# A gated feed-forward block on one core: the down projection from seven block products

## The chip, the cores and the metric

The kernel runs on one core of a Trainium2 chip. The metric is the device time of one execution in microseconds, as the median of several runs. The engines are TensorE (PE, with its weight loads, PEld), VectorE (DVE), ScalarE (ACT), GpSimd (POOL) and SyncE (SP), which here only issues DMAs.

## The reference

A transformer block with 2048 tokens, model width 576 and feed-forward width 4608, all in 32-bit floating point:

```
h = layernorm(x) * (1 + ca) + sa
x = x + ga * attention(h)            # 32 heads of 18, four segments of 512 tokens, with a memory
h = layernorm(x) * (1 + cb) + sb
x = x + gb * ((silu(h @ w_gate) * (h @ w_up)) @ w_down)
```

`sa, ca, ga, sb, cb, gb` are rows of width 576 from `silu(c) @ w_mod`. The change concerns the last line.

## The kernel before, in words

**Products.** Each factor of an accurate product is split in two: a high part (`wh`, `ah`, `dh`, type fp32r) and the remainder (`wl`, `al`, `dl`). A product is then three matmuls: high x high, high x low, low x high. The high part is a cast on ACT, the remainder a subtraction on DVE.

**Stages.** First come layernorm, the projections and the memory. Then attention: 32 units of four heads (segment s, eighth q), as a software pipeline whose order is written out by hand. `PAT` holds four rows (even and odd units, q under 4 and from 4 on) of eleven slots; in each slot the next part of `p2_step` (scores, exponent on ACT, mask on POOL) and of `p1_seq` (row maxima of the unit after the next) is issued, and then the events that the slot names: `V` the product of probabilities and values (`av`), `m` and `n` the transposed maxima, their way through DRAM and `load_m`, `M` the output projection, and so on. `load_stack` on SP's queue brings queries and keys three units ahead.

**Feed-forward.** The 4608 columns are 18 pairs of two blocks of 128. The tokens are worked in two halves of 1024 (t = 0, 1), each as two blocks of 512. For each half and pair, gate (z = 0) and up (z = 1) are a 2x2 by 2x2 block product (two token blocks, two halves of the width 576, two column blocks) made from seven products instead of eight (Strassen and Winograd's form): `y` holds the seven sums of token blocks, `O` the four weight blocks and the three sums that POOL forms from them (`sum_o`), in each half anew. That is 14 steps k per pair. In a step, `prep_w` splits the weights of the step seven ahead, `prod` issues seven matmuls of 512 columns into a PSUM bank of its own (four banks in turn), and DVE adds the banks up (`T[0]`, `T[1]`) and finishes a result (`fin`): for gate ACT applies silu, for up DVE multiplies, and the product is split into `ah`, `al`.

**Down** is plain: `down(t, p, i)` takes token tile i of 128 (eight per half), issues 2 x 6 matmuls of 288 columns with the pair's down weights `dh`, `dl`, and DVE adds the bank to the accumulator `acc[i]`, which was loaded with the residual. Eight such steps for the pair before are issued after products 4 to 11. The down weights are loaded in each half, multiplied by the row gb (`gbB`) on POOL, and split.

**Beside it.** In the first half a second preparation (`prep2`, one yield in each of steps 4 to 13) computes the operands `y` of the second half and keeps them in DRAM (`yD`); at the change of half `load_y` brings each as soon as the last product with the old one has been issued. All DMAs here go through SP's queue, in program order; an engine, too, takes its instructions in program order.

## Time and profile before

| | |
|---|---|
| Time, median of 3 runs | 1944.75 us (1941.69 to 1944.93) |
| Profiled execution, span (the only time the profile has of it) | 1946.8 us |
| PE busy | 1901.2 us |
| PEld busy | 1593.1 us |
| DVE busy | 1533.1 us |
| ACT busy | 824.8 us |
| POOL busy | 1020.6 us |
| Mean granted TensorE clock | 0.993 |

Busy times are sums over stages that differ. A row of a group reads: line, engine, operation, output<-inputs, shapes, count | busy us, mean ns of one | idle time of the engine just before, and what ended it. A row of the timeline reads: start, length, engine, line, operation, count. A matmul's length includes its way through the pipeline, so that the pitch of matmuls is read from their starts.

### The profile page before, as it was taken

How to read it: one execution, taken by the hardware profiler on the slowest of the kernel's cores; microseconds unless marked ns; L12 is line 12 of the kernel's file. 1: busy time of each engine (PE TensorE's matmuls, PEld its weight loads, DVE VectorE, ACT ScalarE, POOL GpSimd, SP SyncE). 2: the span in 40 equal slices, each digit the busy share in tenths (PEclk: the TensorE clock that was granted, in tenths of full speed). 3: DMA queues.
4: the chain of work that ended last, by engine and by line, in shares of the span. 5: the costliest groups of instructions: out<-in, count | busy, mean ns of one | idle time of the engine just before them, and what ended most of it. 6: DMA issues, size and time to landing. Idle time of an engine off the chain costs nothing.

```text
span 1946.8 us, 31901 instructions
## 1 busy us (share of the span) xinstructions
PE 1901.2 (98%) x11119; PEld 1593.1 (82%) x11119; DVE 1533.1 (79%) x3218; ACT 824.8 (42%) x1652; POOL 1020.6 (52%) x1396
## 2 busy tenths in 40 slices
PE   7999999999999899999999999999999999999999
PEld 4887865676766678888888888888888888888888
DVE  6575257878786999898898988979888888878886
ACT  2222256767667434344344343433333333333332
POOL 5322235455544866556565565556565564655551
PEclk9999999999999899999999999999999999999999
DMA  7776564444443332232222222174211211112111
GB/s 207 244 227 233 203 204 140 131 139 150 136 128 125 92 135 101 89 106 80 80 106 83 82 84 78 60 264 146 74 62 45 74 62 59 60 62 74 62 57 50
DMA packets 114354, 223.59 MB, mean 115 GB/s; under 512 B 22992, under 2 KB 40784, under 8 KB 112720
## 3 DMA queue, kind: packets, MB, share of 16 engines
q1 hardware_dynamic: 111936, 215.61, 34.2%
q0 software_dynamic: 576, 5.11, 0.7%
q8 instruction: 88, 1.44, 0.3%
q10 hardware_dynamic: 1680, 0.82, 0.2%
q14 instruction: 74, 0.61, 0.1%
HBM read 161.11 MB, written 60.36 MB: 114 GB/s over the span
## 4 chain that ended last, share of the span: by engine, by line
PE 88%; DVE 4%; DMA 4%; ACT 1%; issue 1%; POOL 1%; SPq 1%; POOLq 0%; ACTq 0%; DVEq 0%
PE M L1090 39%; PE pd L1152 23%; PE pp L93 4%; PE s L576 4%; PE av L596 4%; PE s L174 4%; PE pv L93 3%; PE pw L694 2%; DMA O<-in_wgu_dram 1%; DMA mD<-mr 1%; PE pn L765 1%; PE pm L429 1%; PE px L617 1%; PE pr L346 1%; DVE y L923 1%
## 5 line engine op out<-in xcount | busy, mean ns | idle before, releaser
L1090 PE MATMUL M<-y,wh 128*128 128x512 f32 x2520 | 792.0, 393 | 5.0 <-DVE cu L1106 2.1
L1090 PEld LDWEIGHTS M<-y,wh 128*128 128x128 f32 x2520 | 473.7, 188 | 101.7 <-issue 3.9
L1067 POOL TENSOR_TENSOR wh<-O,wh 32x128 fp32r<-32x128 f32 x504 | 296.6, 593 | 423.0 <-ACT wh L1065 271.3
L1090 PE MATMUL M<-y,wl 128*128 128x512 f32 x1008 | 394.7, 392 | 0.0
L1059 POOL TENSOR_TENSOR O<-O 128x384 f32<-128x384 f32 x288 | 315.4, 1095 | 75.0 <-DMA O<-in_wgu_dram 42.9
L1152 PE MATMUL pd<-dh,ah 128*128 128x288 f32 x1152 | 340.3, 295 | 0.2 <-DVE acc L1155 0.2
L1152 PE MATMUL pd<-dl,ah 128*128 128x288 f32 x1152 | 340.3, 295 | 0.0
L1152 PE MATMUL pd<-dh,al 128*128 128x288 f32 x1152 | 340.1, 295 | 0.0
L1110 ACT CAST ah<-sg 128x512 fp32r<-128x512 f32 x144 | 89.5, 621 | 547.8 <-DVE sg L1107 422.0
L1155 DVE TENSOR_TENSOR acc<-acc,pd 128x576 f32<-128x576 f32 x288 | 216.5, 752 | 111.8 <-PE pd L1152 108.4
L1066 DVE TENSOR_TENSOR wl<-O,wh 128x256 fp32r<-128x256 f32 x504 | 286.2, 568 | 6.0 <-ACT wh L1065 5.2
L179 DVE CUSTOM_DVE_ANT_0 junk<-s,tri 128x256 bf16<-128x256 f32 (+3 forms) x512 | 228.7, 487 | 77.2 <-PE s L174 69.8
L1065 ACT CAST wh<-O 128x384 fp32r<-128x384 f32 x504 | 242.8, 507 | 0.0
L1152 PEld LDWEIGHTS pd<-dl,ah 128*128 128x128 f32 x1152 | 217.4, 189 | 11.8
L1152 PEld LDWEIGHTS pd<-dh,ah 128*128 128x128 f32 x1152 | 216.7, 188 | 11.6 <-DVE acc L1155 0.6
L579 ACT ACTIVATE Pt<-s 128x512 f32<-128x512 f32 (+1 forms) x352 | 186.5, 559 | 88.1 <-PE s L576 72.0
L1152 PEld LDWEIGHTS pd<-dh,al 128*128 128x128 f32 x1152 | 216.6, 188 | 0.0
L1090 PEld LDWEIGHTS M<-y,wl 128*128 128x128 f32 x1008 | 190.0, 188 | 29.6
L1102 ACT ACTIVATE sg<-sg 128x512 f32<-128x512 f32 x144 | 91.2, 633 | 222.7 <-DVE sg L1101 222.7
L576 PE MATMUL s<-qs,ks 110*128 110x512 f32 (+2 forms) x384 | 150.5, 409 | 5.7 <-DMA qs<-mD 4.4
L174 PE MATMUL s<-ks,qs 108*128 108x256 f32 (+3 forms) x512 | 141.2, 327 | 3.3 <-DMA ks<-kD 1.4
L583 POOL TENSOR_SCALAR_AFFINE_SELECT Pt<-Pt 128x512 f32<-128x512 f32 x128 | 81.6, 648 | 100.6 <-ACT Pt L579 100.2
(428 smaller groups left out, 2836.6 us busy)
## 6 DMA issues: line engine op xcount, KB each, us to landing
O<-in_wgu_dram SPq DMA_DIRECT2D x72, 768.0 KB
ks<-kD SPq DMA_DIRECT2D x68, 216.0 KB
qs<-qD SPq DMA_DIRECT2D x68, 216.0 KB
kD<-fh SPq DMA_DIRECT2D x16, 512.0 KB
qD<-fh SPq DMA_DIRECT2D x16, 512.0 KB
yD<-st SPq DMA_DIRECT2D x28, 256.0 KB
y<-yD SPq DMA_DIRECT2D x7, 1024.0 KB
wml<-in_w_mod_dram SPq DMA_DIRECT2D x24, 216.0 KB
```

The source lines that it names most:

```text
L93: nc.tensor.matmul(ps, lhsT=a, rhs=b, start=(k == 0), stop=(k == 13))
L174: nc.tensor.matmul(bank[:, n * (h - h0):n * (h - h0) + n], lhsT=qst[b][0:108, h, 128 * i:128 * i + 128], rhs=kst[b][0:108, h // 2, 0:n], s ...
L179: nc.vector.tensor_tensor_reduce(junk[:, :n], bank[:, n * (h - h0):n * (h - h0) + n], tri[:, L - n:], 1.0, -3e38, op0=ALU.add, op1=ALU.max ...
L576: nc.tensor.matmul(bank[:, n * (g - h):n * (g - h + w)].rearrange("p (a b) -> p a b", a=w), lhsT=kst[u % NB][0:110, g // 2, 128 * j:128 * ...
L579: nc.scalar.activation(pt[:, h:h + per, :n], bank[:, :n * per].rearrange("p (a b) -> p a b", a=per), AF.Exp, scale=SCALE)
L1059: nc.gpsimd.tensor_tensor(o[:, d], o[:, a], o[:, b], op=op)
L1065: nc.scalar.copy(wh, o)
L1066: later.append(lambda: nc.vector.tensor_tensor(wl, o[:, 0:2], f32(wh[:, 0:2]), op=ALU.subtract))
L1067: later.append(lambda: nc.gpsimd.tensor_tensor(wh[32:64, 2], o[32:64, 2], f32(wh[32:64, 2]), op=ALU.subtract))
L1090: nc.tensor.matmul(bank, lhsT=a, rhs=b, start=(n == 0), stop=(n == 6))
L1152: nc.tensor.matmul(pd[:, h, :288], lhsT=a[:, tk], rhs=w[:, f, sl], start=(k == 0), stop=(k == 5))
L1155: nc.vector.tensor_tensor(o, o, pd[:, :, :288], op=ALU.add)
```

## The change

**Down from seven products.** The four results of a pair (two token blocks, two column blocks) and the four 128x288 blocks of its down weights are combined like gate and up. `sum_a` forms four sums of the results on POOL; `prep_a` splits seven operands instead of four; `prep_d` splits seven weight blocks of 288 columns; `down(t, p, c)` issues 14 chunks of six matmuls of 288 columns, `CH` of them after each step, and each chunk is added by DVE to one of seven accumulators `acc[1..7]`. At the end of a half `comb` adds the seven accumulators up to the four blocks of the output; three of them start from the residual, and the fourth is added to it in `x11`. At the end of the second half all 14 chunks of the last pair and the combining adds follow the last product.

**Weights prepared during attention.** `d_prep` multiplies the down weights by gb and forms their four differences on POOL (two products of 576 columns and four subtractions of 288 for each of 18 pairs), and stores the seven blocks to DRAM (seven stores on SP's queue). It goes on by one POOL instruction at each event `W`; the stores follow the last one. Both halves load the seven blocks ready made (`load_d`).

**Sums kept.** In the first half `store_o` writes the sums in `O` to DRAM; the second half loads them (`load_o`) instead of forming them.

**Chained in PSUM.** Products 1, 6, 7 and 4 accumulate in one bank A, 5 and 3 in C; ACT copies A after product 1 into bank B, where product 2 is added, and after 6 and 7 to SBUF (`tb`, `tc`). DVE adds only where a result joins C with `tb` or `tc`. The order of products becomes 1, 5, 6, 2, 7, 4, 3, weights are split five steps ahead, and the last weight rows of all seven products are split at once (`prep_r`).

Moreover the stores of v go from POOL's queue to ACT's, the memory set aside for POOL's DMA descriptors shrinks, and `prep2` has one staging buffer `st` instead of two and transposes into a bank of down.

```diff
-WR = 10
+WR = 7
+PF = 5
+NSG = 8
+CH = (1, 1, 1, 1, 2, 1, 0, 1, 1, 1, 1, 2, 1, 0)
+KS = (0, 1, 2, 3)
+KA = ((5, 2), (6, 4), (7, 6), (3, 8))
...
-                nc.gpsimd.dma_start(vD[s], vs[s])
+                nc.scalar.dma_start(vD[s], vs[s])
...
+    def d_prep():
...
+        for p in range(NF // 2):
+            if p + 1 < NF // 2:
+                load(p + 1)
+            r = R.pop(p)
+            for i in range(2):
+                v = r[:, 2 * i:2 * i + 2].rearrange("p a b -> p (a b)")
+                nc.gpsimd.tensor_tensor(v, v, gbB, op=ALU.mult)
+                yield
+            for d, a, b in ((4, 1, 0), (5, 3, 4), (7, 2, 5), (6, 3, 1)):
+                nc.gpsimd.tensor_tensor(r[:, d], r[:, a], r[:, b], op=ALU.subtract)
+                if d != 6:
+                    yield
+            for i, m in enumerate(POS):
+                nc.sync.dma_start(wdD[p][:, i], r[:, WSLOT[m]])
+            yield
...
+        if n == "W":
+            if s == 3 or (a == "" if q < 4 else a == "0"):
+                next(gd, None)
...
-    MO7 = (1, 2, 6, 7, 4, 5, 3)
+    MO7 = (1, 5, 6, 2, 7, 4, 3)
...
-            st = x2p.tile([P, 2, 256], F32R, tag="st", name="st", bufs=2)
+            st = x2p.tile([P, 2, 256], F32R, tag="st", name="st")
...
+    def step(z, m):
+        if m == 1:
+            B["A"] = ps.tile([P, L], F32, tag="A", name="A", bufs=2)
+            B["B"] = ps.tile([P, L], F32, tag="B", name="B", bufs=1)
+        elif m == 5:
+            B["C"] = ps.tile([P, L], F32, tag="C", name="C", bufs=1)
+        bank = B["B" if m == 2 else "C" if m in (5, 3) else "A"]
+        prime = "set" not in B
+        prod(z, m, bank, m in (1, 5) or m == 2 and prime, m in (2, 4, 3))
...
+                nc.scalar.copy(B["B"], bank)
...
+            copy_t("tb", bank)
...
+            copy_t("tc", bank)
+            fin(z, (1, 1), B["C"], T["tc"])
...
+    def down(t, p, c):
+        m, c = POS[c // 2], c % 2
+        ah, al = AP[p % 2, m]
+        dh, dl = DP[p % 2, m]
+        pd = ps.tile([P, 2, L], F32, tag="dn", name="pd", bufs=2)
+        for i in range(2):
+            tk = slice(128 * (2 * c + i), 128 * (2 * c + i) + 128)
+            for k, (a, w) in enumerate(((ah, dh), (ah, dl), (al, dh))):
+                nc.tensor.matmul(pd[:, i, :288], lhsT=a[:, tk], rhs=w, start=(k == 0), stop=(k == 2))
+        o = acc[m][:, 2 * c:2 * c + 2]
...
+            nc.vector.tensor_tensor(o, o, pd[:, :, :288], op=ALU.add)
...
+                            down(*prev, chunk)
+                            if prev == (0, NPR - 1) and chunk % 2 and POS[chunk // 2] in (2, 5, 6, 7, 3):
+                                comb(0, POS[chunk // 2], None, nc.gpsimd if POS[chunk // 2] in (2, 5) else nc.vector)
...
+        flush()
+        sum_a(0)
+        sum_a(1)
+        prep_a(prev[1] % 2, 5, PA[1, 1])
+        flush()
+        sum_a(2)
+        sum_a(3)
+        for c in range(14):
+            if c in (2, 4, 6):
+                m = (6, 7, 3)[c // 2 - 1]
+                prep_a(prev[1] % 2, m, PA[ASRC[m]])
+                flush()
+            down(*prev, c)
+            comb(1, POS[c // 2], c % 2, nc.vector)
```

More of the change, by code (lines that the diff above doesn't have):

```diff
@@ L1087, in prod @@
                for k in range(2) for a in range(3)]
-        ops.append((wh[0:96, 2], y[0:96, o, 4]))
+        ops.append((R[z][0:96, SLOT[m]], y[0:96, o, 4]))
         for n, (a, b) in enumerate(ops):
-            nc.tensor.matmul(bank, lhsT=a, rhs=b, start=(n == 0), stop=(n == 6))
-        return bank
-    T, SG, AC = {}, {}, {}
+            nc.tensor.matmul(bank, lhsT=a, rhs=b, start=(first and n == 0), stop=(n == 6),
+                             skip_group_check=not first)
+    T, SG, AC, AP = {}, {}, {}, {}
@@ L1121, in step, with comb, ad @@
+    def comb(t, m, c, eng):
+        s_ = slice(0, 4) if c is None else slice(2 * c, 2 * c + 2)
+        def ad(d, b, e=None):
+            (e or eng).tensor_tensor(d[:, s_], d[:, s_], b[:, s_], op=ALU.add)
+        if m == 2:
+            ad(acc[2], acc[1])
+            store(t, 0, 0, acc[2], c)
+        elif m == 5:
+            ad(x11[t], acc[5])
         elif m == 6:
-            nc.vector.tensor_tensor(T[0], bank, T[0], op=ALU.add)
+            ad(acc[6], acc[1])
+            ad(acc[5], acc[6])
@@ L1141, in down @@
[L1141 to L1158 removed]
+            ad(acc[7], acc[6])
@@ L1160, in block @@
+            ad(acc[4], acc[7])
+            store(t, 1, 0, acc[4], c)
+            ad(x11[t], acc[7])
+            store(t, 1, 1, x11[t], c)
+        elif m == 3:
+            ad(acc[3], acc[5])
+            store(t, 0, 1, acc[3], c)
     with tc.manual_schedule():
```

278 lines of the change are left out of this document (172 added, 106 removed), and 6 rows, old and new, of the table PAT.

## The prediction

> **What bounds the kernel now.** I read the page's totals and chain first, then the windows, to see which engine is full in which stage, and last the timeline of a block pair, for the pitch of the instructions.
>
> ```profile
> span 1946.8 us, 31901 instructions
> ...
> PE 88%; DVE 4%; DMA 4%; ACT 1%; issue 1%; POOL 1%; SPq 1%; POOLq 0%; ACTq 0%; DVEq 0%
> ...
> L1152 PE MATMUL pd<-dh,ah 128*128 128x288 f32 x1152 | 340.3, 295 | 0.2 <-DVE acc L1155 0.2
> ...
> 268.00:618.00 350.00, 343.96 (x2522) 231.67 (x2521) 273.03 (x1140) 250.77 (x507) 180.58 (x357) 0.99 0.44 131
> 700.00:1260.00 560.00, 560.00 (x3101) 495.78 (x3100) 490.64 (x786) 222.16 (x458) 333.68 (x407) 1.00 0.26 85
> ...
> 1330.00:1900.00 570.00, 570.00 (x3130) 504.20 (x3129) 465.18 (x747) 210.12 (x422) 322.78 (x389) 1.00 0.19 67
> ```
>
> The last three rows are windows: length, then busy time of PE, weight load, DVE, ACT and POOL, granted clock, DMA share, GB/s. They are attention, the first token half of the feed-forward part and the second. In both halves PE has work in every microsecond at full clock, and down's matmuls waited 0.2 us in all. DVE comes next: 490.64 of 560 in the first half.
>
> ```profile
> 1702.22 0.40 PE L1090 MATMUL M<-y,wh 128*128 128x512 f32 x1
> ...
> 1703.83 0.30 PE L1152 MATMUL pd<-dh,ah 128*128 128x288 f32 x1
> ...
> 1713.42 0.30 PE L1152 MATMUL pd<-dh,ah 128*128 128x288 f32 x1
> ...
> 1715.02 0.40 PE L1090 MATMUL M<-y,wh 128*128 128x512 f32 x1
> ...
> 1748.70 0.30 PE L1152 MATMUL pd<-dh,ah 128*128 128x288 f32 x1
> ```
>
> First column: start. One product (7 matmuls of 512) takes 1703.83-1702.22 = 1.61 us. Twelve down matmuls of 288 take 1715.02-1713.42 = 1.60, so 0.133 each. The rows at 1713.42 and 1748.70 are a pair's last down step and the next pair's: 35.3 us, which is 14x1.61 + 8x1.60 = 35.3. There is no gap in a pair: fewer matmuls shorten it directly, as long as nothing else becomes late.
>
> **Down from seven products.** A pair goes from 96 down matmuls to 84 (14 chunks of 6); gate/up keeps 98. 12x0.133 = 1.6 us a pair, x36 = **-57.6 us**. A pair then needs 14x1.61 + 14x0.80 = 33.7 us of PE.
>
> ```profile
> 1702.42 0.76 DVE L1155 TENSOR_TENSOR acc<-acc,pd 128x576 f32<-128x576 f32 x1 [0.16 <-PE pd L1152]
> 1703.09 0.42 DVE L1066 TENSOR_TENSOR wl<-O,wh 128x256 fp32r<-128x256 f32 x1
> ...
> 1719.61 0.69 DVE L1111 TENSOR_TENSOR al<-sg,ah 128x512 fp32r<-128x512 f32 x1 [0.41 <-ACT ah L1110]
> 1720.22 0.68 DVE L1106 TENSOR_TENSOR cu<-M,tx 128x512 f32<-128x512 f32 x1
> 1720.94 0.69 DVE L1107 TENSOR_TENSOR sg<-cu,sg 128x512 f32<-128x512 f32 x1
> ```
>
> From start to start DVE pays 0.67 for an accumulation, 0.61 for 512 columns, and 0.72 where the next one needs the result. Chaining in PSUM takes ten adds of 512 from DVE (-6.1). Down adds six accumulations (+4.0), three splits al (+1.8) and splits of 7x288 instead of 2x576 weight columns (about +0.9, an estimate at 0.67 per 576 plus starts). Net +0.6 us a pair. From the windows (490.64/560 and 465.18/570 of 35.3) DVE goes from 30.9 to 31.5 and from 28.8 to 29.4 of 33.7: 94% and 87%. It stays below PE, with little room in the first half.
>
> The room is smallest at a pair's end. In steps 11 to 13 DVE gets about 3.4, 2.6 and 2.6 us of work while PE takes 3.2, 2.4 and 1.6, and so comes out 1.4 us behind. Next to need it is the matmul that opens bank C two steps on, 1.61+0.80 = 2.4 us after the last product. That covers 1.4, not much more. In the first half the second operand preparation runs besides: its one staging buffer instead of two can hold ACT for a store, and its loads stand behind the new stores of weight sums (2x768 KB a pair). I take +6 us for the kernel; bounds 0 and 25 (0 as in the 0.2 us of waits above; 25 is 1.4 us, the whole lag, in each of 18 pairs). ACT rises from 222.16/560x35.3 = 14 us to about 22, an estimate from rows of 0.5 to 0.6 us, and isn't near 33.7.
>
> **Weights prepared during attention.** Nearest rows: a product with a gate row, a POOL tensor op of 288 columns, and the end of a unit on POOL and PE.
>
> ```profile
> L873 POOL TENSOR_TENSOR woraw<-woraw,gaB 128x576 f32<-128x576 f32 x5 | 7.1, 1422 | 1.2 <-DMA woraw<-in_wo_dram 1.0 <-issue 0.2
> ...
> L634 POOL TENSOR_TENSOR o<-o,tmp 128x288 f32<-128x288 f32 x23 | 18.5, 802 | 40.4 <-DVE tmp L633 40.4
> ...
> 465.09 0.20 POOL L187 TENSOR_SCALAR mc<-ml 128x16 fp32r<-128x16 f32 x1
> ...
> 466.34 0.29 PE L193 MATMUL pmt<-ident,mc 128*32 128x128 f32 x1
> ...
> 448.37 0.24 SPq L161 DMA_DIRECT2D qs<-mD  x1
> ...
> 451.62 0.29 SPq L157 DMA_DIRECT2D ks<-kD  x1
> 451.96 0.37 SPq L158 DMA_DIRECT2D qs<-qD  x1
> ...
> 452.70 0.50 PE L576 MATMUL s<-qs,ks 110*128 110x512 f32 x1
> ```
>
> POOL gets 18x(2x1.42 + 4x0.80) = 109 us: 181 becomes 290 of 350, so the stage still fits. Queued behind each op is the mask of the score tiles, and PE's av waits for that. In 16 of the units an op stands between the last two masks, ahead of mc; mc ended at 465.29 and PE read it at 466.34. Against this 1.05 us an op of 0.80 costs nothing, one of 1.42 costs 0.37: 0 to 6 us in all. On SP's queue each of 18 bursts of seven stores waits for POOL's last subtraction, then takes 7x0.34 = 2.4 us to issue (start to start, as at 451.62); queued behind it are load_stack and load_m, for which the next unit's first scores wait. Only 4 of the 18 bursts stand straight ahead of a load_m. The first scores began about 4.3 us after the row at 448.37 (the 512-column matmul at 452.70), so such a burst costs between nothing and some 4 us: 0 to 15. Of 0 to 21 I take **+5**. The four stores of v that go from POOL's queue to ACT's I cost at nothing: no engine's row waits for them. The DMA engines have room: 18x(576 KB loaded + 1,008 KB stored) adds 83 GB/s to the 131 that took a share of 0.44, so about 0.72 (an estimate in proportion). In feed-forward the loads of the ready weights and sums add some 50 to 60 GB/s to shares of 0.26 and 0.19: nothing, by the same proportion.
>
> ```profile
> 1275.37 0.33 SPq L1041 DMA_DIRECT2D y<-yD  x1
> ...
> 1296.82 12.68 DMA O<-in_wgu_dram
> ...
> PE M L1090 <- DMA y<-yD: 0.6, 2, 0.3
> ...
> y<-yD SPq DMA_DIRECT2D x7, 1024.0 KB
> ...
> y<-yD SPq DMA_DIRECT2D x7, 192.0 KB
> ...
> O<-in_wgu_dram SPq DMA_DIRECT2D x72, 768.0 KB
> ```
>
> **Change of half.** From 1275.37 to 1296.82+12.68 = 1309.50 seven operand loads (8,512 KB) and two O tiles landed: 10,048 KB in 34.1 us, 301 GB/s. After the change one O tile of 1,344 KB (sums included) joins the seven: 33.5 us. The last operand is needed 12 products and 14 chunks after the first load is issued, at 12x1.61+14x0.80 = 30.5 us: 3.0 us late, against 0.6 waited before: +2.4. Then the first half's results are put together, with six whole-tile adds of 1,152 columns on DVE: 6x2x0.67 = 8 us in a pair with 4.3 to spare; I take 5.6. Together **+8**, bounds 2 and 14.
>
> **The tail.**
>
> ```profile
> 1942.53 0.29 PE L1152 MATMUL pd<-dh,al 128*128 128x288 f32 x1
> ...
> 1942.86 0.76 DVE L1155 TENSOR_TENSOR acc<-acc,pd 128x576 f32<-128x576 f32 x1 [0.84 <-PE pd L1152]
> ...
> L753 POOL TENSOR_TENSOR pq<-qe,qf 128x512 f32<-128x512 f32 (+1 forms) x15 | 19.2, 1282 | 2.8 <-ACT qf L745 2.7
> ...
> L1110 ACT CAST ah<-sg 128x512 fp32r<-128x512 f32 x144 | 89.5, 621 | 547.8 <-DVE sg L1107 422.0
> ```
>
> Before, DVE ends 0.8 us after PE. After the change all 14 chunks of the last pair follow the last product, and DVE has more to do there than PE's 11.2 us. In order: add and multiply (1.4), POOL's sum (1.28), ACT's split (0.62), al (0.61), 4.1 us with handovers; then 14 accumulations (9.4), 16 combining adds that each need the result before (0.67+0.12, 12.6) and three al (1.8): 27.9 us. The excess over PE is 16.7 instead of 0.8: **+16**, bounds 12 (the lead hidden) and 18.
>
> **Sum.** -57.6+6+5+8+16 = -22.6. The span, 1946.8, is the only time of the profiled execution, and 2 us above the runs' median, 1944.75; 22.6 off the median is **1922 us**. With every term at its bound: -43.6 (1901) and +20 (1965). About 0.2%, 4 us, is what a measurement of this kernel can tell.
>
> **Rivals.**
>
> ```profile
> L923 DVE TENSOR_TENSOR y<-h,y 128x512 fp32r<-128x512 f32 x6 | 8.2, 1423 | 0.0
> ...
> L1111 DVE TENSOR_TENSOR al<-sg,ah 128x512 fp32r<-128x512 f32 x144 | 104.8, 728 | 23.5 <-ACT ah L1110 22.9
> ```
>
> *DVE becomes the bound of the first half* (the other side: slower). The same subtraction of two SBUF tiles took 1423 ns beside a crowded POOL and 728 elsewhere; accumulations, which read PSUM, show no such spread. The change swaps ops of the second kind for the first. If the seven al and seven half-width dl took the longer time, DVE's pair would grow by 4.9+2.4 to 38.8. It bites from 33.7 on. At half of that growth, 35.2, 18 pairs lose 18x1.5 = 27 us, and 1922+27-5 (stalls that the sum holds already) = 1944, level with before; with all of it 2009. I price it between, at 1975. Against it: POOL's work in a pair doesn't grow (14 tails and two products go, four sums come), and 728 is the mean under it. The Trainium skill says why (SBUF — State Buffer, SBUF: two separate sides): GpSimd and a DVE instruction with two SBUF inputs lock each other out for a whole instruction. The two rows agree with it. By the rule alone each of the fourteen could wait out a POOL sum, and this rival would be the forecast.
>
> *Attention loses what feed-forward gains.* If all 18 bursts cost 2.4 to issue plus 1,008 KB at 301 GB/s (3.4), less half of the 4.3 us, that is 3.7x18 = 66: 1983. It decides from 1.3 us a burst. Against it: 14 bursts do not stand before a load_m.
>
> *Chained banks wait for ACT.* PE can't write bank A until ACT has copied it; between products 7 and 4 stand two chunks, 1.6 us, against a copy of about 0.6. If ACT is late by 1.5 us in each half-pair, 72x0.5 = 36: 1958. ACT is two thirds busy, which speaks against it.
>
> *The change does less than it says*: 84 matmuls at the same pitch are certain from their shape, so this has no chance of its own.
>
> **Chances.** Forecast 0.68 (1907 to 1938), DVE 0.12, attention 0.10, banks 0.05, anything else 0.05. Faster: 0.68 and the mild third of the others, 0.78; same 0.06; slower 0.16. Range 1904 to 1948: the forecast, and the near half of the rivals.
>
> **What would show it.** Right: a pair of 33.7 to 34.2 us in both halves, PE busy throughout, a DVE tail of 28 us after the last product, attention within 10 us of 350. Wrong: waits of down's matmuls for acc in the first half (DVE), of scores for qs (attention), of gate/up for tb, tc or B (banks).

## The result, and the profile after

The time rose from 1943.8 us (median; 1941.7 to 1944.9) to **2117.8 us** (2113.2 to 2119.4): a ratio of 1.089, interval 1.087 to 1.091. The forecast was 1922 us, and the range ended at 1948.

By stages of the two profiled executions, from the starts of the first and last matmul of each stage:

| stage | before, us | after, us | difference |
|---|---|---|---|
| start, to the first av | 268.6 | 272.7 | +4.1 |
| attention, first to last av | 349.8 | 405.0 | **+55.2** |
| to the first gate/up product | 40.8 | 43.8 | +2.9 |
| first half, to the 19th pair | 633.8 | 704.0 | **+70.2** |
| second half, to the last gate/up matmul | 639.9 | 657.4 | +17.5 |
| from there to the end | 13.9 | 34.5 | +20.6 |

In all kernels below the start took between 260 and 276 us, for no cause that was looked for. So stages are compared rather than totals where microseconds count.

The page of the changed kernel, its span, its chain and two of its costly groups:

```profile
span 2117.4 us, 31191 instructions
...
DVE 44%; PE 34%; DMA 9%; issue 6%; ACT 4%; POOL 2%; SPq 0%; ACTq 0%; DVEq 0%; POOLq 0%
...
L1244 PE MATMUL pd<-dh,ah 128*128 128x288 f32 x1008 | 316.7, 314 | 70.7 <-DVE acc L1249 67.9
...
L585 PE MATMUL s<-qs,ks 110*128 110x512 f32 (+2 forms) x384 | 157.1, 426 | 35.4 <-DMA qs<-mD 32.6
```

The chain was 88% PE and is now 44% DVE. Down's matmuls waited 0.2 us for accumulations and now wait 67.9; scores wait 32.6 us for the row maxima to come back from DRAM. The windows of attention, before and after, and of the two halves after, with the columns that the prediction explains:

```profile
268.60:618.40 349.80, 343.76 (x2529) 231.56 (x2528) 272.50 (x1138) 250.32 (x506) 180.76 (x357) 0.99 0.44 130
...
272.70:677.70 405.00, 366.62 (x2524) 241.98 (x2528) 277.15 (x1136) 250.25 (x502) 283.71 (x464) 0.94 0.60 180
830.00:1300.00 470.00, 429.76 (x2203) 363.12 (x2201) 450.69 (x633) 232.73 (x519) 247.58 (x191) 0.97 0.39 132
1470.00:2040.00 570.00, 552.95 (x2861) 466.83 (x2862) 519.92 (x788) 284.90 (x630) 161.21 (x96) 0.99 0.31 109
```

DVE is 96% busy in the first half and 91% in the second: 38.4 and 32.8 us of work a pair (450.69/470x40.0 and 519.92/570x36.0), where the forecast had 31.5 and 29.4. In the second half it is not full. PE waits where DVE comes late, and DVE's accumulations in their turn waited 25.0 us of that window for PE. A pair took 40.0 us in the first half (mean of 16) and 36.0 in the second, where 33.7 was forecast. Pair lengths here and below are worked out from the starts of a pair's first accumulation and the next pair's. The timeline of one pair of the second half shows what happens:

```profile
1726.46 0.42 DVE L1121 TENSOR_TENSOR wl<-O,wh 128x256 fp32r<-128x256 f32 x1
1726.71 4.47 POOL L1212 TENSOR_TENSOR sg<-sg 128x512 f32<-128x512 f32 x3 [10.31 <-DVE sg L1166]
1726.79 1.55 DVE L1133 TENSOR_TENSOR dl<-dr__18871,dh 128x288 fp32r<-128x288 f32 x1
1728.27 1.77 DVE L1206 TENSOR_TENSOR al<-sg,ah 128x512 fp32r<-128x512 f32 x1
1729.97 0.74 DVE L1249 TENSOR_TENSOR acc<-acc,pd 128x576 f32<-128x576 f32 x1
...
1730.76 0.40 PE L1244 MATMUL pd<-dh,ah 128*128 128x288 f32 x1 [0.58 <-DVE acc L1249]
...
1731.82 2.11 POOL L1109 TENSOR_TENSOR wr<-O,wr 32x896 fp32r<-32x896 f32 x1 [0.64 <-PE pd L1244]
1732.05 2.17 DVE L1121 TENSOR_TENSOR wl<-O,wh 128x256 fp32r<-128x256 f32 x1
...
1762.74 4.47 POOL L1212 TENSOR_TENSOR sg<-sg 128x512 f32<-128x512 f32 x3 [10.31 <-DVE sg L1166]
```

wl takes 0.42 us when it starts ahead of POOL's sums and 2.17 when it starts 0.23 us after a POOL operation of 2.11: it ends 0.29 us after that one. dl and al, issued as POOL's sums start, take 1.55 and 1.77. The accumulation, which reads PSUM, takes 0.74 beside the same sums. Then PE stands waiting for an accumulation. The last row is the same sum one pair later: 36.03 us.

Attention, around one late round trip of the maxima, with the granted clock behind it:

```profile
383.50 0.31 ACTq L207 DMA_DIRECT2D mD<-mr  x1
...
388.07 0.85 PE L605 MATMUL av<-Pt,vq 128*32 128x384 f32 x8
...
390.00 0.23 SPq L170 DMA_DIRECT2D qs<-mD  x1
...
392.06 0.47 PE L585 MATMUL s<-qs,ks 110*128 110x512 f32 x1 [3.14 <-DMA qs<-mD]
...
393.19 0.63 PE L183 MATMUL s<-ks,qs 108*128 108x512 f32 x1
```

```profile
392.00:394.00 2.00, 1.94 (x8) 1.12 (x12) 0.84 (x3) 1.17 (x2) 2.00 (x2) 0.60 0.90 308
394.00:396.00 2.00, 2.00 (x14) 0.60 (x10) 0.55 (x2) 0.43 (x2) 0.23 (x1) 0.54 0.97 306
396.00:398.00 2.00, 2.00 (x20) 1.72 (x21) 1.60 (x5) 1.60 (x4) 0.45 (x1) 1.00 0.50 157
```

The store of the maxima is issued at 383.50 and their load only at 390.00, when the store has landed: 6.5 us for 16 KB. This trip, from the issue of the small store to the issue of its load, took 5.0 us on average over 30 units, 2.9 before. The DMA packets in the trace show where the time goes: the last of the store's 48 packets ends 4.2 us after the issue on average (2.3 before), and the load is issued 0.8 us after that (0.6 before). So it is the store that comes late, and not SP. PE waits 3.14 us, and for the next 4 us the granted clock is 0.60 and 0.54.

So a wait is paid twice. Of the 55.2 us, 32.4 are idle time of PE (405.0-366.6 against 349.8-343.8) and 22.9 are the same matmuls at a lower clock (366.6 against 343.8 busy). The trace's clock record has half clock for 51.4 us of attention, against 4.4 before; half of the difference is 23.5, which is about the 22.9. In the first half of the feed-forward part it has 36.2 us, against none before, so that up to 18 of the 70.2 us there are the clock's as well.

The Trainium skill (TensorE: Matmul & The Clock Gate, Part 1: The HAM clock gate) has a gate that falls to half after about 3.4 us of idleness and needs as long to open. Here the spells of half clock behind such waits last 3.41 or 6.83 us, which agrees; but 1.6 us of idleness already brought one on (the spell that starts at 648.41 us), which is less than the page has, and the measurement decides.

The tail, DVE and POOL after the last product (which ends at 2083.3):

```profile
2085.80 6.04 POOL L1212 TENSOR_TENSOR sg<-sg 128x512 f32<-128x512 f32 x4 [26.13 <-DVE sg L1166]
...
2085.95 3.42 DVE L1206 TENSOR_TENSOR al<-sg,ah 128x512 fp32r<-128x512 f32 x2
...
2101.50 1.55 DVE L1254 TENSOR_TENSOR acc<-acc,acc 128x576 f32<-128x576 f32 x2
...
2113.28 0.76 DVE L1254 TENSOR_TENSOR acc<-acc,acc 128x576 f32<-128x576 f32 x1
```

DVE ends at 2114.0, 30.7 us after the product (27.9 forecast); two of the splits al stand beside POOL's sums and take 3.42 us.

### The profile page after: what moved, and what is told of

Its sections match the earlier page's. It is cut to its first block, busy times and chain, and to the rows that moved or that the text cites. A ratio compares the mean times of both kernels' runs of the same rounds, so it can differ in the third digit from the quotient of the medians.

```text
span 2117.4 us, 31191 instructions
## 1 busy us (share of the span) xinstructions
PE 1931.2 (91%) x10687; PEld 1558.6 (74%) x10687; DVE 1747.7 (83%) x3385; ACT 1012.6 (48%) x2156; POOL 935.2 (44%) x998
## 4 chain that ended last, share of the span: by engine, by line
DVE 44%; PE 34%; DMA 9%; issue 6%; ACT 4%; POOL 2%; SPq 0%; ACTq 0%; DVEq 0%; POOLq 0%
DVE wl L1121 10%; DVE acc L1249 9%; PE A L1143 7%; DVE dl L1133 7%; DVE al L1206 6%; DMA mD<-mr 5%; PE pd L1244 5%; PE C L1143 4%; PE pp L99 4%; PE pv L99 3%; PE s L585 3%; DVE cu L1165 2%; DVE sg L1162 2%; PE av L605 2%; PE s L183 2%
## 5 line engine op out<-in xcount | busy, mean ns | idle before, releaser
L1143 PE MATMUL A<-y,wh 128*128 128x512 f32 x1152 | 410.0, 396 | 7.5 <-ACT tc L1171 6.1
L1249 DVE TENSOR_TENSOR acc<-acc,pd 128x576 f32<-128x576 f32 x488 | 357.4, 743 | 35.6 <-PE pd L1244 35.4
L1244 PE MATMUL pd<-dh,ah 128*128 128x288 f32 x1008 | 316.7, 314 | 70.7 <-DVE acc L1249 67.9
L1212 POOL TENSOR_TENSOR sg<-sg 128x512 f32<-128x512 f32 x144 | 203.9, 1416 | 313.8 <-DVE sg L1166 285.7
L1109 POOL TENSOR_TENSOR wr<-O,wr 32x896 fp32r<-32x896 f32 x72 | 158.8, 2205 | 388.3 <-ACT wr L1108 328.0
L1143 PEld LDWEIGHTS A<-y,wh 128*128 128x128 f32 x1152 | 218.9, 190 | 51.4 <-ACT tc L1171 7.6
L1206 DVE TENSOR_TENSOR al<-sg,ah 128x512 fp32r<-128x512 f32 x252 | 231.1, 917 | 29.2 <-ACT ah L1205 28.9
L1143 PE MATMUL A<-y,wl 128*128 128x512 f32 x576 | 228.6, 397 | 0.0
L1143 PE MATMUL C<-y,wh 128*128 128x512 f32 x576 | 211.4, 408 | 15.7 <-DVE cu L1165 14.4
L1244 PEld LDWEIGHTS pd<-dl,ah 128*128 128x128 f32 x1008 | 193.6, 192 | 16.7
L1114 POOL TENSOR_TENSOR O<-O 128x384 f32<-128x384 f32 x144 | 163.7, 1152 | 80.7 <-DVE acc L1249 40.6
L1120 ACT CAST wh<-O 128x256 fp32r<-128x256 f32 x504 | 198.8, 402 | 0.0
L585 PE MATMUL s<-qs,ks 110*128 110x512 f32 (+2 forms) x384 | 157.1, 426 | 35.4 <-DMA qs<-mD 32.6
```

The lines of the kernel that those rows point to most:

```text
L585: nc.tensor.matmul(bank[:, n * (g - h):n * (g - h + w)].rearrange("p (a b) -> p a b", a=w), lhsT=kst[u % NB][0:110, g // 2, 128 * j:128 * ...
L1114: nc.gpsimd.tensor_tensor(o[:, d], o[:, a], o[:, b], op=op)
L1120: nc.scalar.copy(wh, o)
L1143: nc.tensor.matmul(bank, lhsT=a, rhs=b, start=(first and n == 0), stop=(n == 6), skip_group_check=not first)
L1206: later.append(lambda: nc.vector.tensor_tensor(al, src, f32(ah), op=ALU.subtract))
L1212: nc.gpsimd.tensor_tensor(PA[d], PA[a], PA[b], op=op)
```

## The experiments

Theory A: POOL's operations lengthen DVE's operations on two SBUF operands, and DVE so becomes what a pair takes. Rival B: the single banks and down's two. Rival C: the operands wait for POOL's sums. For attention, where the first runs have an A and a B of their own, it is the transfers, POOL's operations, or SP's order. All results together; attention and pair lengths are from the profiled executions.

| kernel | median, us | ratio to before (interval) | attention | pair, first half | pair, second half |
|---|---|---|---|---|---|
| before | 1943.8 | | 349.8 | 35.7 | 35.3 |
| changed | 2117.8 | 1.089 (1.087 to 1.091) | 405.0 | 40.0 | 36.0 |
| 1 no preparation | 2057.4 | 1.058 (1.057 to 1.060) | 349.4 | 40.1 | 36.0 |
| 2 its POOL part alone | 2077.9 | 1.068 (1.066 to 1.070) | 361.1 | 40.1 | 36.0 |
| 3 its transfers alone | 2101.8 | 1.081 (1.079 to 1.084) | 397.6 | 40.2 | 36.0 |
| 4 no sums, no tails | 2032.1 | 1.045 (1.043 to 1.047) | 400.7 | 37.1 | 34.1 |
| 5 no dl | 2030.7 | 1.045 (1.042 to 1.048) | 398.9 | 37.4 | 33.8 |
| 6 sums that nobody reads | 2115.1 | 1.087 (1.085 to 1.089) | 402.5 | 40.0 | 36.0 |
| 7 as 4, and no weight sums | 2000.3 | 1.029 (1.027 to 1.030) | 400.5 | 35.6 | 34.1 |
| 8 as 4, two buffers | 2022.7 | 1.041 (1.039 to 1.042) | 400.6 | 36.7 | 34.1 |
| 9 sums on DVE | 2090.4 | 1.075 (1.073 to 1.077) | 398.3 | 39.3 | 35.2 |
| 10 stores spread | 2103.7 | 1.084 (1.080 to 1.087) | 388.3 | 40.0 | 36.0 |
| 11 floor | 1932.0 | 0.994 (0.992 to 0.995) | 351.0 | 35.1 | 34.1 |
| 12 three remedies | 2074.4 | 1.067 (1.065 to 1.068) | 390.3 | 39.0 | 35.2 |
| 13 half the columns | 2086.3 | 1.073 (1.071 to 1.076) | 381.7 | 40.2 | 36.0 |
| 14 half the rows | 2106.4 | 1.084 (1.081 to 1.086) | 401.8 | 40.2 | 36.0 |
| 15 behind the load of maxima | 2126.2 | 1.093 (1.090 to 1.095) | 411.0 | 40.3 | 36.0 |
| 16 stores on ACT's queue | 2136.7 | 1.099 (1.094 to 1.103) | 428.1 | 40.3 | 36.0 |
| 17 stores alone | 2082.2 | 1.071 (1.066 to 1.075) | 376.2 | 40.1 | 36.0 |
| 18 POOL in short pieces | 2040.1 | 1.049 (1.047 to 1.050) | 404.5 | 37.6 | 34.1 |

Kernels whose attention code is that of the changed one (4 to 9 and 18) took 398 to 405 us for it: differences of a few us there mean nothing.

### What lengthened attention

**1, no preparation.**

```diff
-        gd = d_prep()
+        gd = iter(())
...
-        nc.sync.dma_start(r, wdD[p])
+        nc.sync.dma_start(r[:, 0:2].rearrange("p a b -> p (a b)"), wd[2 * p])
+        nc.sync.dma_start(r[:, 2:4].rearrange("p a b -> p (a b)"), wd[2 * p + 1])
+        nc.sync.dma_start(r[:, 4:6].rearrange("p a b -> p (a b)"), wd[2 * p])
+        nc.sync.dma_start(r[:, 6], wd[2 * p + 1][:, 0:288])
```

> The changed kernel without any preparation of the down weights during attention: the events that drive it do nothing, and feed-forward loads the plain weight blocks of the pair into the seven slots (four loads for one), so the product with gb and the four differences are left out. If the preparation is what lengthened attention, the stage from the first to the last av goes from 405.0 us back to 345 to 355, scores wait under 8 us for qs (32.6 in the changed kernel), and the time falls by about 50 us to 2060 to 2070. Rival: the changed pools and buffers or the stores of v on ACT's queue lengthened attention; then it stays above 390. Feed-forward should stay at 39.8 and 36.0 us a pair under each theory.

**2 and 3, its halves.**

```diff
 2: -                nc.sync.dma_start(wdD[p][:, i], r[:, WSLOT[m]])     # and the loads after the first two
 3: -                nc.gpsimd.tensor_tensor(v, v, gbB, op=ALU.mult)
    -                nc.gpsimd.tensor_tensor(r[:, d], r[:, a], r[:, b], op=ALU.subtract)
```

> Of the preparation only POOL's six operations a pair are kept, on two buffers loaded once; the loads and the stores to DRAM are left out, and feed-forward loads the plain blocks as in the first experiment. Theory A, that the bulk transfers and the issues on SP's queue hold up the small round trip of the row maxima (store, load) for which the next scores wait: attention 350 to 360 us, scores wait under 10 us for qs, the time about 2065 to 2075. Theory B, that POOL's operations stand ahead of the masks and of mc: attention 385 to 405, the time 2100 to 2118. A mixture shows as a number between.

> Of the preparation only the DMAs are kept (two loads and seven stores a pair, at the same events, of the plain blocks); POOL's six operations a pair are left out. Theory A (transfers and issues hold up the small round trip): attention 390 to 405 us, waits for qs near 30 us, the time 2100 to 2118. Theory B (POOL): attention 350 to 360, the time 2065 to 2075. A third: SP itself waits for POOL's last subtraction ahead of a burst, with load_m queued behind; then neither half alone shows it, and both this and the run with POOL alone come out below 365.

One window each, without preparation, with POOL's part and with the transfers:

```profile
263.90:613.30 349.40, 343.50 (x2525) 231.42 (x2528) 272.40 (x1140) 250.46 (x506) 181.18 (x357) 1.00 0.44 131
```

```profile
276.30:637.40 361.10, 349.18 (x2524) 234.47 (x2528) 278.59 (x1136) 249.42 (x502) 283.72 (x464) 0.98 0.42 124
```

```profile
266.60:664.20 397.60, 360.08 (x2529) 238.93 (x2528) 274.46 (x1140) 251.71 (x506) 181.22 (x357) 0.95 0.64 189
```

Attention returns to 349.4 without preparation, so all of its growth was that. POOL's operations cost 11.7 us and the transfers 48.2; the two together come to 59.9 against 55.6 measured. Theory A of these two runs (the transfers) holds for most of it, B (POOL's operations) for a fifth. The third, that SP waits for POOL ahead of a burst, needs both halves together and falls, since the transfers alone cost 48.2. The trip of the maxima takes 2.9 us without preparation, 2.7 with POOL's part and 4.8 with the transfers.

**10, the stores spread** over the six events of a pair:

```diff
-            for i, m in enumerate(POS):
-                nc.sync.dma_start(wdD[p][:, i], r[:, WSLOT[m]])
+                put(p, r, sl)       # one store at each event, two at the last
```

> The changed kernel with the seven stores of the preparation spread over the six events of a pair (one at each, two at the last, none waiting for an operation of the same event), and the next load issued two events after the last store of its buffer; POOL's operations and the bytes are the same. If the burst of seven stores on SP's queue and in the DMA engines is what held up the round trip of the row maxima: waits for qs fall from 32.6 us to under 12, attention from 405 to 362 to 378 (with POOL's operations alone it took 361), the time by 25 to 43 us. If it is the bytes as such, whenever they go: attention 390 to 405, the time within 15 us of 2117.

Neither range was met: attention is 388.3, the waits for the maxima fall only from 32.6 to 23.6 us, and the trip still takes 4.8. The burst was a part of it, 16.7 us, and not the main thing.

**13 and 14, half of each transfer; 17, stores alone; 16, the stores on ACT's queue** (all on top of 3), and **15, the transfers behind the load of the maxima**:

```diff
 13: +                nc.sync.dma_start(wdD[p][:, i, 0:144], r[:, i % 2 * 2, 0:144])
 14: +                nc.sync.dma_start(wdD[p][0:64, i], r[0:64, i % 4])
 17: -                load(p + 1)                      # two buffers, loaded once
 16: +                nc.scalar.dma_start(wdD[p][:, i], r[:, i % 4])
 15:                  load_m(u + 1, (u + 1) % NB)
     +                if pend:
     +                    pend.pop(0)()                # seven stores, then the load two pairs on
```

> The run with the transfers alone (no POOL operations; attention 397.6 us, mean time from the issue of the small store of the maxima to the issue of their load 4.8 us, against 349.4 and 2.9 without preparation), with half the columns in each of the nine transfers a pair: as many issues and as many packets, half the bytes in each. Feed-forward loads the plain blocks. If bytes hold up the round trip: attention 368 to 380 us, round trip 3.5 to 4.1. If packets or issues do: 390 to 398 and 4.5 to 4.8.

> The run with the transfers alone, with 64 of the 128 partitions in each of the nine transfers a pair: as many issues, half the packets and half the bytes. If bytes or packets hold up the round trip: attention 368 to 380 us. If the issues on SP's queue do (nine a pair, about 0.4 us each): 390 to 398. If half the columns won nothing and this does, it is the packets.

> The changed kernel with the preparation's transfers (seven stores of a finished pair and the load of the pair after the next) issued together straight behind a load of the maxima, instead of at the events of POOL's operations; nothing is left out. If what counts is what is still under way when the next small store is issued, about 9 to 10 us later: mean round trip 3.0 to 3.8 us instead of 5.0, waits for qs under 14 us instead of 32.6, attention 362 to 378 us, the time 2080 to 2100. If it is the bytes wherever they go: round trip 4.5 to 5, attention 388 to 405.

> The run with the transfers alone (no POOL operations; attention 397.6 us), with the seven stores a pair on ACT's queue instead of SP's; loads and all bytes as there, feed-forward loads the plain blocks. If the transfers cost by being in the DMA engines: attention 390 to 405 us, round trip of the maxima 4.3 us or more. If they cost by their place in SP's queue: 355 to 372 us, and SP's waits for keys, queries and stores ahead of them are gone.

> The run with the transfers alone, without the two loads a pair: the seven stores go on from two buffers loaded once (1008 of 1584 KB a pair). If the bytes decide, about a third of the 48 us goes: attention 378 to 386. If SP's waits ahead of a load (for the stores of its buffer to land) or the loads themselves decide: under 370. If only the stores count: 392 to 400.

Half the bytes in rows half as long win 15.9 of 48.2 us, and a third of the bytes left out (the loads) wins 21.4. Bytes would do something like that, though 381.7 lies just above the range that I had given for them and 376.2 just below it. Half the bytes as half the rows win nothing (401.8), which bytes and packets would not do. The trip is shorter even there, 4.3 us instead of 4.8 (4.6 with half the columns, 4.3 without the loads); but five of the loads of the maxima then let their scores start only 4.4 to 7.6 us after the load's issue, instead of about 2. So the load can come late as well as the store.

The two moves, 15 and 16, show new waits instead, and attention lies outside both ranges of each. With the transfers behind the load of the maxima (15) the trip does fall, to 3.7 us as expected, but SP waits for the stores to land before it can issue the next load of weights, and masks come late on PE (19.2 us, from 11.4), for a reason that no run separates:

```profile
PE s L585 <- DMA qs<-mD: 22.4, 11, 6.0
PE av L605 <- POOL Pt L592: 19.2, 7, 9.1
...
SPq L826 <- DMA wd<-dq: 25.9, 32, 2.4
```

With the stores on ACT's queue (16) the waits for the maxima fall to 9.0 us, from 28.9 in 3, and the trip to 3.2, but ACT's exponents stand behind the stores, and the scores wait 40.9 us for ACT, from 2.4:

```profile
ACT Pt L588 <- DMA wd<-dq: 56.7, 18, 4.2
```

So it is settled that the transfers cost four fifths of attention's growth, and that it comes as waits for the maxima, whose store moves late, and as lowered clock after them. What about a transfer delays the small store and its load is not settled: neither bytes, packets nor the place in SP's queue accounts for all of these runs.

### What lengthened the pairs

**4, no sums, no tails.**

```diff
-                            if k == KS[j]:
-                                sum_a(j)
...
-        later.append(lambda: nc.gpsimd.tensor_tensor(r[32:64], ..., op=ALU.subtract))
```

> The changed kernel without POOL's four sums of results a pair (the operands are split from the results themselves) and without POOL's subtraction for the last weight rows: POOL does nothing in the second half, and in the first only the weight sums and the second operand preparation. DVE's instructions are the same in number. Theory A (DVE sets the pair, because its operations with two SBUF inputs are lengthened by POOL's): in the second half al falls from 856 ns to about 690, dl from 884 to about 450, the pair from 36.0 to 33.7 to 34.3 us; in the first half the pair falls from 39.8 to 36 to 38; the time to about 2030 to 2060. Rival B (the single banks B and C and the two banks of down, whatever the length of DVE's operations): the pair stays at 35.5 to 36.0, the time at 2105 to 2118.

Its second half, where POOL does nothing: the window, two groups of DVE, and ACT's cast for the last weight rows in two pairs in turn.

```profile
1470.00:1980.00 510.00, 510.00 (x2725) 444.25 (x2724) 402.26 (x750) 270.56 (x598) 0.00 (x0) 1.00 0.32 111
```

```profile
L1120 DVE TENSOR_TENSOR wl<-O,wh 128x256 fp32r<-128x256 f32 x210 | 87.6, 417 | 0.0
L1205 DVE TENSOR_TENSOR al<-sg,ah 128x512 fp32r<-128x512 f32 x105 | 72.0, 685 | 15.0 <-ACT ah L1204 13.2
```

```profile
1710.76 0.94 ACT L1108 CAST wr<-O 96x896 fp32r<-96x896 f32 x1
...
1744.85 0.94 ACT L1108 CAST wr<-O 96x896 fp32r<-96x896 f32 x1
```

PE is busy in every microsecond, the pair takes 34.1 us, wl 417 ns (595 in the changed kernel) and al 685 (856). The same DVE instructions need 402.26/510x34.1 = 26.9 us a pair instead of 519.92/570x36.0 = 32.8. With the same banks the second half now runs at PE's own pace: rival B falls.

**5, no dl.**

```diff
-        later.append(lambda: nc.vector.tensor_tensor(dl, r, f32(dh), op=ALU.subtract))
-        DP[p % 2, m] = (dh, dl)
+        DP[p % 2, m] = (dh, dh)
```

> The changed kernel without DVE's seven subtractions dl a pair; the matmuls of high operand and low weight read the high weight instead, so PE's work is the same, and POOL's too. Theory A (DVE's throughput sets the pair, with its operations lengthened by POOL's): the pair loses up to 7x0.88 = 6.2 us of DVE work, so the second half falls from 36.0 to 33.9 to 34.5 us a pair and the first from 39.8 to 36 to 37.5; the time falls by 80 to 110 us. Rival C (the pair waits for POOL's four sums, that is for the operands split from them, and the run without the sums took away that wait): the second half stays at 35.6 to 36.0.

33.8 and 37.4 us a pair, with POOL's work whole: less DVE work does the same as less POOL work, as theory A has it.

```profile
L1204 DVE TENSOR_TENSOR al<-sg,ah 128x512 fp32r<-128x512 f32 x106 | 114.8, 1083 | 15.1 <-ACT ah L1203 13.1
```

al now takes 1083 ns: it comes to stand where dl stood, and waits out the sum in its place.

**6, sums that nobody reads**, in pairs 4 to 17 of the second half.

```diff
-        nc.gpsimd.tensor_tensor(PA[d], PA[a], PA[b], op=op)
+        nc.gpsimd.tensor_tensor(scr[0], PA[a], PA[b], op=op)
```

> The changed kernel, but in pairs 4 to 17 of the second half POOL writes its four sums a pair into a buffer that nobody reads, and the operands are split from the results themselves, as in the run without sums. POOL's and DVE's operations are the same in number and size; only the wait for POOL's results is gone. The first half is the control (39.8 us). Theory A (POOL lengthens DVE's operations): the second half stays at 35.7 to 36.1 us a pair, al at 800 to 860 ns, the time within 6 us of 2117. Rival C (a wait for the sums): 34.1 us a pair as without sums, the time near 2090.

```profile
L1206 DVE TENSOR_TENSOR al<-sg,ah 128x512 fp32r<-128x512 f32 x84 | 70.6, 840 | 10.5 <-ACT ah L1205 10.5
```

The pair stays at 36.03 us with no one waiting for a sum. Rival C falls.

**7, the weight sums left out as well, and 8, two staging buffers**, both on top of 4.

```diff
 7: -        nc.gpsimd.tensor_tensor(o[:, d], o[:, a], o[:, b], op=op)    # and store_o; plain blocks are loaded
 8: -            st = x2p.tile([P, 2, 256], F32R, tag="st", name="st")
    +            st = stb if cnt[0] % 2 else x2p.tile([P, 2, 256], F32R, tag="st", name="st")
```

> The run without POOL's sums of results and without its subtraction for the last weight rows, and now also without the sums of weights in the first half and their stores: O's three sum slots are loaded with plain blocks (768 and 576 KB a tile). What is left on POOL in the first half is the second operand preparation. Against 37.1 us a pair in the first half of the run without sums of results: if the weight sums still lengthen DVE's operations (wl 496 ns there against 417 in its second half), wl falls to about 420 and the first half to 34.8 to 35.8 us; if the single staging buffer of the second operand preparation is what is left (ACT waited 29.6 us in 470 for its stores), the first half stays at 36.3 to 37.1.

> The run without POOL's sums of results and without its subtraction for the last weight rows, and the second operand preparation with two staging buffers in turn again (the second lies in an unused half of another tile). If the one buffer costs the first half its last microseconds: ACT's waits for the stores of st fall from 29.6 us in 470 to under 5, and the first half falls from 37.1 to 35.3 to 36.2 us a pair, the time by 15 to 30 us from 2032. If they are idle time that costs nothing: 36.8 to 37.1, the time within 5 us of 2032.

```profile
L1115 DVE TENSOR_TENSOR wl<-O,wh 128x256 fp32r<-128x256 f32 x167 | 70.4, 421 | 0.2
```

Without the weight sums wl in the first half takes 421 ns as in the second, and the pair falls from 37.1 to 35.6 us. Two buffers take away ACT's waits for the stores of st (34.2 us in a window of 420), but win only 0.45 us a pair and 9.4 us in all: most of that idle time cost nothing, and the lower end of what I expected (15 us) was too high.

**9, the sums on DVE.**

```diff
-        nc.gpsimd.tensor_tensor(PA[d], PA[a], PA[b], op=op)
+        nc.vector.tensor_tensor(PA[d], PA[a], PA[b], op=op)
```

> The changed kernel with the four sums of results a pair on DVE instead of POOL; everything is computed. By the windows of the second half POOL's sums and tails cost DVE 519.92/570x36.0 - 402.26/510x34.07 = 32.8 - 26.9 = 6 us a pair in lengthened operations. On DVE the four sums take about 4x0.72 = 2.9 us themselves, and POOL's two tails stay. Theory A: DVE then needs 31 to 33 us, so the second half falls from 36.0 to 34.1 to 35.2 us a pair, the first, where POOL's weight sums stay, from 40.0 to 38 to 39.5; the time falls by 30 to 70 us. Rival: DVE pays for the sums as much as it saves, 35.5 to 37 us, the time within 15 us of 2117.

35.2 and 39.3 us, within what theory A gave, though the time fell by 27.4 us, a little under the 30 to 70 expected: DVE pays for the sums with most of what it saves.

**18, POOL's work in short pieces.** What stayed open is why the kernel before, with POOL busy 322.78 of 570 us in its second half, did not suffer, and the changed one with 161.21 does. A part of the answer is room. DVE's wl was lengthened there too (547 ns, against 417 undisturbed), but DVE had only 28.8 us of work in a pair of 35.3. The other part is that POOL's operations were shorter: sums of 1.1 us and tails of 0.6, beside two products of 1.5 in a pair. The sums and tails of before come first, then those of after.

```profile
L1059 POOL TENSOR_TENSOR O<-O 128x384 f32<-128x384 f32 x130 | 141.2, 1086 | 22.4 <-DMA O<-in_wgu_dram 10.9 <-DVE ty L1125 2.6
L1067 POOL TENSOR_TENSOR wh<-O,wh 32x128 fp32r<-32x128 f32 x227 | 136.1, 604 | 224.7 <-ACT wh L1065 145.3 <-DVE wl L1066 42.2 <-PE M L1090 29.2
```

```profile
L1212 POOL TENSOR_TENSOR sg<-sg 128x512 f32<-128x512 f32 x64 | 90.9, 1420 | 177.2 <-DVE sg L1166 173.5
L1109 POOL TENSOR_TENSOR wr<-O,wr 32x896 fp32r<-32x896 f32 x32 | 71.0, 2219 | 246.8 <-ACT wr L1108 239.9 <-PE pd L1244 3.9 <-DVE acc L1249 3.0
```

```diff
-        nc.gpsimd.tensor_tensor(PA[d], PA[a], PA[b], op=op)
+        for i in range(4):
+            v = slice(128 * i, 128 * i + 128)
+            nc.gpsimd.tensor_tensor(PA[d][:, v], PA[a][:, v], PA[b][:, v], op=op)
...
-        later.append(lambda: nc.gpsimd.tensor_tensor(r[32:64], ..., op=ALU.subtract))
+            for i in range(7):                                     # in one function, put on later
+                nc.gpsimd.tensor_tensor(r[32:64, i], ..., op=ALU.subtract)
```

> The changed kernel with each of POOL's four sums of results cut into four operations of 128 columns, and its subtraction for the last weight rows cut into seven of 128 columns: the same elements, in operations of about 0.4 to 0.6 us instead of 1.4 and 2.2; nothing is left out. If what DVE loses is set by the length of the single operation that it has to wait out: in the second half wl falls from 600 ns to 480 to 560 and al from 840 to 700 to 780, the pair from 36.03 to 34.2 to 35.4 us, the time by 15 to 50 us. If the amount of POOL's work sets it (the pieces come to more of it, through their fixed cost): wl and al stay or grow, the pair is 35.8 to 37 us, the time within 15 us of 2117 or above.

```profile
1470.00:1980.00 510.00, 510.00 (x2726) 444.19 (x2725) 432.06 (x749) 270.06 (x600) 232.55 (x448) 1.00 0.33 115
```

```profile
L1125 DVE TENSOR_TENSOR wl<-O,wh 128x256 fp32r<-128x256 f32 x210 | 98.1, 467 | 0.0
L1210 DVE TENSOR_TENSOR al<-sg,ah 128x512 fp32r<-128x512 f32 x105 | 83.2, 793 | 13.1 <-ACT ah L1209 13.1
...
L1218 POOL TENSOR_TENSOR sg<-sg 128x128 f32<-128x128 f32 x238 | 129.3, 576 | 125.9 <-DVE sg L1170 124.7
```

POOL is busier (232.55/510x34.1 = 15.5 us a pair against 161.21/570x36.0 = 10.2), and yet the second half takes 34.1 us a pair, as if POOL did nothing, and the time falls by 78 us to 2040, more than the 15 to 50 expected. DVE needs 432.06/510x34.1 = 28.9 us a pair, 2.0 more than without POOL instead of 5.9. The single times are not quite as expected: wl fell further (467 ns), al less (793). So what DVE loses here is set mostly by the length of the operation that it has to wait out, and not by POOL's amount of work. It is the largest gain of a kernel here that leaves nothing out. The first half stays at 37.6 us a pair; POOL's weight sums there, 1.15 us each, were left whole, and no run cut them.

### What the form could reach

**11, floor**: 1 and 7 and 8 together. **12**: 8's buffers, 9 and 10 together, which leaves out nothing.

> What the seven-product form could reach if its preparations cost nothing: no preparation of the down weights in attention (plain blocks are loaded), no sums of weights or of results, no subtraction for the last weight rows on POOL, and two staging buffers in the second operand preparation; PE's work is whole. From the single runs, 2117.8 - 60.4 (no preparation) - 117.5 (no sums) - 9.4 (two buffers) = 1930 us if the stages add up, that is 14 us below the kernel before: attention 349, pairs of 35.3 and 34.1 us, the rest the tail and the change of half. If what is saved in one place turns up in another, 1945 to 1960.

> The three remedies that leave out nothing, together: the sums of results on DVE, the stores spread, two staging buffers. If they add up to the sum of their single effects (sums 30 to 70 us, stores 25 to 43, buffers about 9) the time is 1995 to 2055, still above the kernel before at 1944, because POOL's weight sums in the first half, its operations during attention and the tail remain.

The floor is 1932.0 us against 1930 expected, so the costs of the stages add up; it lies 0.6% under the kernel before, and leaves out work that the result needs. The three remedies together won 43 us, less than their 51 singly (27.4, 14.1 and, on top of 4, 9.4), and less than I had expected, because 9 and 10 had been expected too high. 18 was not run together with 8 and 10. No kernel that computes the whole came below the kernel before.

## Why the prediction was wrong, point by point

**What bounds the kernel, and fewer matmuls.** PE was the bound, and where nothing else disturbs it (4, second half) the pair is 34.1 us at full clock: 1.2 us less than 35.3, not 1.6. Over 36 pairs the first term is -44 instead of -57.6 us. The matmuls of 288 columns kept their pitch of 0.133 us; those of 512 start 0.232 us apart instead of 0.229 (means of the second half), for a reason that no run was made for.

**Stalls in the pairs, +6 (0 to 25): the step that failed.** Against 34.1 us, 18 pairs of 40.0 and 18 of 36.0 cost about 106 and 34 us, of which the kernel before had some 7 already (18 pairs of 35.7 against 35.3). The prediction took DVE's prices from start-to-start distances in the old kernel (0.61 for al) and carried them over unchanged: 31.5 and 29.4 us of DVE work a pair, 94% and 87%. The runs show 38.4 and 32.8 in their place. It held against its own rival that POOL's work in a pair doesn't grow; that is true (161.21 of 570 after, 322.78 before) and does not matter. Two long kinds of operation, 1.4 and 2.2 us, took the place of tails of 0.6 and, in the second half, of sums of 1.1, and POOL's sums start when DVE has finished sg (the rows at 1726.71 and 1726.79), just as dl and al stand next on DVE. The work on DVE without POOL, 26.9 us a pair in the second half, was even less than the forecast's 29.4. That waits of PE also lower its clock (36.2 us at half clock in the first half) was not in the sum either.

**The rival of DVE as the bound** (0.12, 1975, up to 2009) was the mechanism, by its own rows: its 38.8 us of DVE work a pair is near the 38.4 of the first half. But it was priced for the first half alone; the second half, with POOL busy 161.21 of 570 us, loses as well. The Trainium skill's rule that the prediction cites there (SBUF — State Buffer, SBUF: two separate sides), of a lock held for a whole instruction, agreed with the timeline (wl 2.17 us beside 2.11) and was the better guide: by it alone this rival would have been the forecast.

**Weights prepared during attention, +5 (0 to 21): it failed too**, at +55. POOL's operations, bounded at 6, cost 11.7. For the transfers only the bursts straight ahead of a load_m were counted, as time on SP's queue, and at 2.4 us each; the 18 bursts took 3.3 to 10.5 us to issue, 4.9 on average. That the transfers slow the small store and its load themselves was missing, and so was the lower clock after each wait (22.9 us). The rival's 66 us for attention was near by luck: its sum has every burst holding up SP, and not the store.

**Change of half, +8 (2 to 14): right in size, in part by luck.** The three intervals at the change took 117.2 us against 3x36.0, so +9, and +0.3 before. The combining adds were the cause as forecast: 9.3 us of DVE's time, and behind them PE waited 3.9 us for accumulations and 3.8 for cu. But no product waited for its operands y, where 3.0 us had been counted.

**The tail, +16 (12 to 18): a little over its bound.** The stage grew by 20.6; 1.6 of that is down work that stood ahead of the last product before (14 chunks of 0.80 follow it now, 6 steps of 1.60 did), so in the sum's terms it is +19. The sequence of operations was right. DVE ended 2.8 us later than forecast; the two splits beside POOL's sums (3.42 us instead of 1.2) are most of that, and the handovers were not separated.

**Chained banks waiting for ACT** (0.05): products in bank A waited 6.1 us in all for ACT's copy tc, so it was rightly low. Those in bank C waited 14.4 us for DVE, which belongs to the stalls above. *The change does less than it says* got no chance, rightly for the count of matmuls, though these pay 44 us at best, and the floor keeps 12 of them beside the tail, the change of half and a slower first half.

## What to carry to other kernels

Before work is moved to POOL, look for DVE operations on two SBUF operands that will be issued at the same moment, and price each at up to the length of the whole POOL operation; then cut POOL's operations short, which here was worth 78 us for a few changed lines. A stage with DMA capacity to spare can still have a small round trip on its path: transfers added beside it cost the wait and, behind the wait, a slower TensorE clock. And when the bound engine has been full to the last microsecond, the saving has to be set against the work of the second engine with its contention, not with its prices from the old schedule.

## What the runs showed of the hardware

A POOL operation on only 32 partitions (wr, 2.2 us) holds up a DVE operation on 128 as one on all partitions does (wl 2.17 us instead of 0.42). DVE operations with one operand in PSUM showed no lengthening (accumulations 742 to 754 ns on average in every window read). Seven transfers of 144 KB put on ACT's queue made ACT wait up to 4.2 us at a time, 56.7 us in all. Transfers over 64 partitions with half the bytes cost attention as much as those over 128 (401.8 and 397.6 us). The spells of half TensorE clock that began in attention lasted 3.41 or 6.83 us, and in the 3.41 us before each of them PE had been idle for between 1.2 and 3.41 us.
